# Loading one of twelve streamed weight blocks over eight DMA engines instead of sixteen

## The chip, the cores and the metric

The kernel runs on one core of a Trainium2 chip. The metric is the device time of one execution in microseconds; the time of a kernel is the median of its runs. The core has a matrix engine (PE), a vector engine (DVE), a scalar engine (ACT), a general engine (POOL), an engine that mainly issues transfers (SP), and sixteen DMA engines that move data between memory and the on-chip buffers for all of them.

## The reference, cut to what matters

Two independent parts are computed, and their outputs stand side by side in one output of 2048 rows and 2048 columns. Part A is an attention layer that runs over 64 segments one after the other, because each hands eight memory rows to the next. Part B is a long convolution by a state space model; the change doesn't touch it.

```python
for s in range(n_seg):                       # 64 segments of 32 rows
    xs = x[:, s * seg_len:(s + 1) * seg_len, :]
    h = concatenate([mem, xs], axis=1)       # 8 memory rows, 32 rows; 1024 wide
    q, k, v = (einsum('btd,dhe->bhte', h, W) for W in (Wq, Wk, Wv))   # 32 heads of 128
    p = softmax(where(mask, einsum('bhqe,bhke->bhqk', q, k) * scale, -1e9))
    o = einsum('bhte,hed->btd', einsum('bhqk,bhke->bhqe', p, v), Wo)
    mem = o[:, :8, :]
    outs.append(o[:, 8:, :])
```

The four weights Wq, Wk, Wv and Wo have 1024 x 4096 values each, 8 MB in bf16, and every segment needs all of them.

## The kernel before, in words

Part B runs first, to about 590 us. Beside it the kernel projects those rows of part A that no segment hands on, copies some weights, and loads others for good. Then part A's loop (`part_a`, `for s in range(NS)`) runs over the 64 segments.

The weights are cut into 64 blocks of 128 x 2048 values (512 KB). A key names a block: `("k", 0, 2)` is the third block of rows of the first half of Wk's columns, and `("o", 13)` holds rows 26 x 128 to 28 x 128 of Wo, that is two heads. Most blocks stay in on-chip memory for the whole loop (`W_res`), a few are kept in a bank for matmul results (`KEPT`), and twelve are read from memory again in every segment (`STREAM` and `STREAM_O`): three of k, two of q, four of v, and the output blocks 4, 8 and 13. In order of use a segment streams k(0,2), q(0,2), k(1,1), k(1,5), q(1,4), v(0,2), v(0,7), v(1,4), v(1,7), o4, o8, o13.

Streamed blocks are read from a copy in memory (`WD`), which `streamed_copies` makes once, during part B, as a contiguous 128 x 2048 array. `part_a.stage` (line 337) takes one of four buffers (`wst`, `SLOTS = 4`) in turn and issues the load on SP (line 340). The schedule is the program's order, written out by hand. SP goes ahead of the other engines in that order, so a load is issued as soon as SP has issued the one before it and PE has finished with the block that had the same buffer, four blocks earlier.

`unit(key)` (line 300) returns a block to whoever multiplies by it. `quads` (line 414) does the projections: four matmuls of 512 columns a block, on four groups of 32 columns of PE. `oproj` (line 527) does the output projection: eight matmuls of 256 columns a block. Block o13 is the last but one in the order of the final call, `oproj(pp[:, 1, :], (8, 10, 12, 14, 9, 11, 13, 15), o1)`, and the next streamed block after it is k(0,2), the second block of the next segment's k projection.

ACT issues the small transfers of a segment: `load_pk` (line 376) and `load_vx` (line 382), and in `stores` a 64 KB part to `OLd` (line 392) and the segment's 64 KB of output rows (line 396). The latter store writes through a view of four column groups (`"r (q d) -> q r d"`), so that its outermost size is 4.

After the loop, line 647 loads the output blocks that aren't resident once more, for the matmuls of line 664.

Of the kernel before, what the change touches and what calls it, by code (L numbers as in the profile page):

```python
# [10 lines left out]
BF16 = mybir.dt.bfloat16  # L11
# [13 lines left out]

STREAM = {("k", 0): (2,), ("q", 0): (2,), ("k", 1): (1, 5), ("q", 1): (4,), ("v", 0): (2, 7), ("v", 1): (4, 7)}
STREAM_O = (4, 8, 13)

BANK = {("k", 0): "b0", ("q", 0): "b1", ("k", 1): "b2", ("q", 1): "b0", ("v", 0): "b3", ("v", 1): "b2"}
KEPT = {("k", 0, 7): (("K7a", 0, 512), ("K7b", 512, 512), ("K7c", 1024, 512), ("K7d", 1536, 384), (None, 1920, 128)),  # L30
# [28 lines left out]
def streamed_keys():  # L59
    return [key for key in [(m, t, kc) for (m, t), kcs in STREAM.items() for kc in kcs] + [("o", u) for u in STREAM_O]]  # L60


def streamed_copies(ctx, tc, src):
    nc = tc.nc
    dram = ctx.enter_context(tc.tile_pool(name="a_wd", bufs=1, space=bass.MemoryType.DRAM))
    out, copies = {}, []
    for key in streamed_keys():
        t_ = dram.tile([128, 2048], BF16, name="WD_%s" % "_".join(str(i) for i in key))
        copies.append(lambda t_=t_, key=key: nc.sync.dma_start(
            out=t_[:].rearrange("e (h d) -> e h d", h=2) if key[0] == "o" else t_[:], in_=src(key)))  # L70
        out[key] = t_
    return out, copies


class Ahead:
# [3 lines left out]
    def __init__(self, ctx, tc, x, src, seg_len):  # L79
        self.nc, self.tc, self.x, self.src = tc.nc, tc, x, src  # L80
        self.S, self.Dm = x.shape
        self.SL, self.XM = seg_len, 24
        self.XL, self.KC, self.NS = seg_len - 24, self.Dm // 128, self.S // seg_len
        dram = ctx.enter_context(tc.tile_pool(name="a_dram", bufs=1, space=bass.MemoryType.DRAM))
        self.VXd = dram.tile([self.NS + 1, 128, 256 + self.KC * self.XM], BF16, name="VXd")
        self.PKd = dram.tile([self.NS, 128, 512], BF16, name="PKd")
        self.PVd = [dram.tile([self.NS * self.XL, 2048], BF16, name="PVd%d" % t) for t in range(2)]
        self.OLd = dram.tile([self.NS // 8, 128, 8 * 256], BF16, name="OLd")
# [183 lines left out]
def part_a(ctx, tc, x, src, WD, HE, seg_len, out_a, ahead, W_res, rest, places, first):  # L272
    nc = tc.nc
# [26 lines left out]
    def unit(key):  # L300
        if key in rest:

            rest.remove(key)
            load_resident(tc, wres, src, key, W_res, None, places.pop(0)() if places else None)
        if key in W_res:
            return W_res[key]
        if key in KEPT:
            return ahead_of.pop(key) + halves.get(key, [])
        between.pop(key, lambda: None)()
        if key in first:  # L310
            return first.pop(key)
        if key[0] == "v":
            for k_ in rest[0:3 if key[1] == 0 else 1]:
                rest.remove(k_)
                load_resident(tc, wres, src, k_, W_res)
        return stage(key, WD[key][:])

    ctx_l = ctx_w.enter_context(ExitStack())
    pers = ctx_l.enter_context(tc.tile_pool(name="a_pers", bufs=1))
# [14 lines left out]
    def words(out, in_):  # L334
        nc.vector.tensor_scalar(out=out.bitcast(I32), in0=in_.bitcast(I32), scalar1=0, scalar2=None, op0=ALU.bitwise_or)  # L335

    def stage(key, in_):
        t_ = wst.tile([128, 2048], BF16, name="wst", tag="w%d" % (loads[0] % SLOTS))
        loads[0] += 1
        nc.sync.dma_start(out=t_[:].rearrange("e (h d) -> e h d", h=2) if len(in_.shape) == 3 else t_[:], in_=in_)  # L340
        return t_

    def load_kept(key):
# [62 lines left out]
    for s in range(NS):  # L406
# [123 lines left out]
        a = quads("k", 0, (0, 2, 4, 6, 1, 3, 5, 7))  # L530
        k0 = evac(a, "k0")
        a = quads("q", 0, range(0, 6))
# [4 lines left out]
        a = quads("k", 1, range(0, 3))  # L537
# [16 lines left out]
        a = quads("q", 1, range(KC))  # L554
# [3 lines left out]
        a = quads("v", 0, range(0, 3))  # L558
# [34 lines left out]
        a = quads("v", 1, range(0, 5))  # L593
# [46 lines left out]
    wo = {}  # L640
    for u in order:
        if ("o", u) in W_res:
            wo[u] = W_res["o", u]
        else:
            wo[u] = spare.pop(0)
            if ("o", u) in WD:
                nc.sync.dma_start(out=wo[u][:], in_=WD["o", u][:])
            else:
                nc.sync.dma_start(out=wo[u][:].rearrange("e (h d) -> e h d", h=2), in_=src(("o", u)))
    stores(NS - 1, ob)  # L650
# [6 lines left out]
    for b in range(4):  # L657
        pe = [ps_k.tile([128, 512], F32, name="pe", tag="keep%d" % (2 * (b % 2) + n)) for n in range(2)]
        for u in order:
            for hh in range(2):  # L660
                h = 2 * u + hh
                hi = 16 * (h // 16) + 4 * (h % 4) + (h % 16) // 4
# [983 lines left out]
@with_exitstack  # L1646
def kernel(
    ctx: ExitStack,
    tc: tile.TileContext,
    A_x: bass.AP,  # L1650
    A_mem0: bass.AP,
    A_Wq: bass.AP,
    A_Wk: bass.AP,
    A_Wv: bass.AP,
    A_Wo: bass.AP,
    A_seg_len: bass.AP,
    B_u: bass.AP,
    B_A_re: bass.AP,
    B_A_im: bass.AP,
    B_B_re: bass.AP,  # L1660
    B_B_im: bass.AP,
    B_C_re: bass.AP,
    B_C_im: bass.AP,
    B_log_dt: bass.AP,
    B_Dskip: bass.AP,
    out: bass.AP,
):
    seg_len = int(A_seg_len)
    Dm = A_x.shape[2]
    Db = B_u.shape[2]  # L1670
    out_a = out[0, :, 0:Dm]
    out_b = out[0, :, Dm:Dm + Db]
    src = weight_blocks(A_Wq.rearrange("d h e -> d (h e)"), A_Wk.rearrange("d h e -> d (h e)"),
                        A_Wv.rearrange("d h e -> d (h e)"), A_Wo.rearrange("h e d -> (h e) d"))
    WD, copies = streamed_copies(ctx, tc, src)
    ahead = Ahead(ctx, tc, A_x[0], src, seg_len)
    ctx_w = ctx.enter_context(ExitStack())
    W_res, places, first = {}, [], {}
    rest = Keys(RESIDENT)
    rest.ctx = ahead.ctx = ctx_w  # L1680

    def residents(stay, early, uqs, last):
        def put(t_):
            load_resident(tc, None, src, rest.pop(0), W_res, None, t_)
        for _ in range(EARLY[0]):
            load_resident(tc, stay, src, rest.pop(0), W_res)
            yield
        def some(where, tag, n):
            t_ = where.tile([128, n, 2048], BF16, name="W%d" % n, tag=tag)
            return [t_[:, i, :] for i in range(n)]  # L1690
        for t_ in some(stay, "KT1", 2):
            put(t_)
            yield
        for t_ in early:
            put(t_)
            yield
        put(last[0])
        yield
        for t_ in uqs:
            put(t_)  # L1700
            yield
        ahead.wst = ctx_w.enter_context(tc.tile_pool(name="a_wst", bufs=1, side="right"))
        pool = ctx_w.enter_context(tc.tile_pool(name="a_wre0", bufs=1, side="right"))
        for _ in range(EARLY[1]):
            load_resident(tc, pool, src, rest.pop(0), W_res)
            yield
        for i, key in enumerate([("k", 0, 7)] + streamed_keys()[0:SLOTS - 1]):
            first[key] = t_ = ahead.wst.tile([128, 2048], BF16, name="wst", tag="w%d" % i)
            tc.nc.sync.dma_start(out=t_[:], in_=WD[key][:] if key in WD else src(key))
            yield  # L1710
        for i in [c // 2 for c in PAIRS]:
            places.append(lambda i=i: stay.tile([128, 2048], BF16, name="W1", tag="MI%d" % i))
        for i in range(LATE):
            put(places.pop(0)())
            yield
        put(last[1])
        yield

    low = low_blocks(ctx, tc)
    ahead.low = low.pop()  # L1720
    copies += [lambda t_=t_: load_resident(tc, None, src, rest.pop(0), W_res, None, t_) for t_ in low]

    def first_state(m0, xt):
        nc = tc.nc
        consts = constants(tc, ahead)
        hT = next(consts)
        nc.sync.dma_start(out=xt[:].rearrange("p k r -> p (k r)"), in_=ahead.VXd[0, :, 256:])
        nc.sync.dma_start(out=m0, in_=A_mem0[0])
        pm = yield
        for kc in range(8):  # L1730
            nc.tensor.transpose(out=pm[:, kc, :], in_=m0[:, kc * 128:(kc + 1) * 128], identity=ahead.consts[0][0:8, 0:8])
        nc.vector.tensor_copy(out=hT[:, :, ahead.XM:], in_=pm)
        nc.gpsimd.tensor_copy(out=hT[:, :, 0:ahead.XM], in_=xt[:])
        yield
        next(consts)
        yield

    with ExitStack() as ctx_b:
        part_b(ctx_b, tc, B_u[0], B_A_re, B_A_im, B_B_re, B_B_im, B_C_re, B_C_im, B_log_dt, B_Dskip, out_b, ahead, copies, residents, first_state)
    with ExitStack() as ctx_a:  # L1740
        part_a(ctx_a, tc, A_x[0], src, WD, A_Wo.shape[0] * A_Wo.shape[1], seg_len, out_a, ahead, W_res, rest, places, first)
# [35 lines left out]
```

## Time and profile before

| what | value |
|---|---|
| median of 3 runs | 1962.2 us (1956.45, 1962.97, 1962.2) |
| span of the profiled execution, first to last instruction | 1954.2 us |
| the profiled execution's own time | not given apart from its span |
| PE busy | 1810.2 us, 93% |
| DVE, ACT, POOL busy | 71%, 48%, 23% |
| moved by DMA | 591.08 MB, mean 302 GB/s |
| mean granted clock of PE | 0.974 |

Instructions, their engines and their tiles are shown under the line of the kernel that issued them ("L340"). A tile name stands for all buffers of that name: `wst` for the four buffers of streamed blocks, `WD_o` for the copies of the three output blocks, `acc` and `pp` for results of the projections. "SPq" is SP's queue of transfers, q1 holds the transfers that SP issues, q10 those of ACT, q0 those of POOL, and q8 fetches instructions. A line of the page that shows 40 digits cuts the span into 40 slices of 48.9 us, and a digit is the busy share of a slice in tenths.

### The profile page before, as it was taken

How to read it: one execution, taken by the hardware profiler on the slowest of the kernel's cores; microseconds unless marked ns; L12 is line 12 of the kernel's file. 1: busy time of each engine (PE TensorE's matmuls, PEld its weight loads, DVE VectorE, ACT ScalarE, POOL GpSimd, SP SyncE). 2: the span in 40 equal slices, each digit the busy share in tenths (PEclk: the TensorE clock that was granted, in tenths of full speed). 3: DMA queues.
4: the chain of work that ended last, by engine and by line, in shares of the span. 5: the costliest groups of instructions: out<-in, count | busy, mean ns of one | idle time of the engine just before them, and what ended most of it. 6: DMA issues, size and time to landing. Idle time of an engine off the chain costs nothing.

```text
span 1954.2 us, 74192 instructions
## 1 busy us (share of the span) xinstructions
PE 1810.2 (93%) x31750; PEld 1106.9 (57%) x31788; DVE 1379.4 (71%) x3431; ACT 934.7 (48%) x1670; POOL 443.1 (23%) x855
## 2 busy tenths in 40 slices
PE   8999999887997899999999999999999999998998
PEld 3666666556775555555555555555555555555554
DVE  8599989889994566666676766676766676666650
ACT  8799989851122334344434443444444444444320
POOL 2364545223222111111111111111111111111120
PEclk8999999878998999999999999999999999999999
DMA  7889898867589999999999999999999999999991
GB/s 222 243 232 283 237 287 243 221 188 253 169 272 334 347 340 340 340 339 336 355 339 346 345 335 336 339 341 350 344 350 334 347 341 347 339 350 324 338 343 30
DMA packets 337342, 591.08 MB, mean 302 GB/s; under 512 B 94848, under 2 KB 211048, under 8 KB 334964
## 3 DMA queue, kind: packets, MB, share of 16 engines
q1 hardware_dynamic: 284824, 531.85, 79.9%
q10 hardware_dynamic: 45532, 29.57, 4.9%
q0 software_dynamic: 6656, 24.92, 3.5%
q8 instruction: 249, 4.08, 0.8%
q14 instruction: 81, 0.66, 0.1%
HBM read 528.78 MB, written 68.47 MB: 306 GB/s over the span
## 4 chain that ended last, share of the span: by engine, by line
PE 37%; DMA 27%; DVE 4%; issue 1%; ACT 1%; POOL 0%; SPq 0%; ACTq 0%; DVEq 0%; POOLq 0%
PE acc L414 20%; DMA wst<-WD_v 8%; PE pp L527 8%; DMA wst<-WD_o 7%; DMA wst<-WD_k 3%; DMA arena<-PKd 3%; DMA wst<-WD_q 3%; PE pe L664 3%; PE tr L425 2%; DMA out_dram<-arena 1%; DMA out_dram<-uu 1%; PE pv L495 1%; PE pv L499 1%; DVE arena L621 1%; PE sc L439 1%
## 5 line engine op out<-in xcount | busy, mean ns | idle before, releaser
L414 PEld LDWEIGHTS <-a_hT 128*32 128x32 bf16 x12352 | 328.4, 96 | 324.0 <-issue 64.0
L420 ACT CAST arena<-acc 128x512 bf16<-128x512 f32 x384 | 224.8, 585 | 404.3 <-PE acc L414 324.5
L414 PE MATMUL acc<-wst,a_hT 128*32 128x512 bf16 x2304 | 229.5, 382 | 34.2 <-DMA wst<-WD_v 22.9
L527 PEld LDWEIGHTS <-arena 128*32 128x32 bf16 x8256 | 216.1, 96 | 73.2 <-issue 49.3
L335 DVE TENSOR_SCALAR arena<-keep 128x256 int32<-128x256 int32 (+1 forms) x512 | 175.6, 395 | 28.1 <-PE acc L414 28.0
L428 POOL COPY arena<-arena 128x128 bf16<-128x128 bf16 x128 | 37.3, 292 | 683.0 <-DMA arena<-PKd 314.4
L414 PE MATMUL acc<-XM,a_hT 128*32 128x512 bf16 x2560 | 172.7, 380 | 0.0
L458 ACT ACTIVATE sc<-sc 128x160 f32<-128x160 f32 (+1 forms) x192 | 63.9, 333 | 127.6 <-DVE sc L455 127.6
L454 DVE TENSOR_REDUCE a_mx<-sc 128x4 f32<-128x160 f32 (+1 forms) x192 | 71.7, 374 | 74.7 <-PE sc L442 73.3
L197 PE MATMUL pro<-XM,wsl 128*128 128x512 bf16 x480 | 117.7, 383 | 5.3 <-DVE kst L206 2.2
L527 PE MATMUL pp<-W_o,arena 128*32 128x256 bf16 x3584 | 120.6, 273 | 0.1
L414 PE MATMUL acc<-W,a_hT 128*32 128x512 bf16 x1536 | 120.0, 384 | 0.0
L542 DVE COPY arena<-tr 128x512 bf16<-128x512 bf16 x64 | 27.2, 425 | 128.8 <-PE tr L425 128.8
L462 DVE TENSOR_REDUCE a_mx<-sc 128x4 f32<-128x160 f32 (+1 forms) x192 | 72.9, 379 | 55.3 <-ACT sc L458 54.9
L489 POOL TENSOR_TENSOR arena<-arena,a_BD 128x128 bf16<-128x128 bf16 x128 | 51.1, 399 | 231.1 <-DVE arena L472 229.7
L1266 DVE TENSOR_SCALAR nr<-ptt 128x456 f32<-128x456 int16 x128 | 80.4, 628 | 31.8 <-PE ptt L1244 29.0
L1258 ACT ACTIVATE E<-pa 128x648 bf16<-128x648 f32 x128 | 87.7, 712 | 18.1 <-PE pa L1250 16.0
L414 PE MATMUL acc<-wq,a_hT 128*32 128x512 bf16 x1024 | 92.2, 381 | 0.0
L414 PE MATMUL acc<-g,a_hT 128*32 128x512 bf16 x1024 | 90.4, 379 | 0.0
L1459 POOL TENSOR_TENSOR Bt<-ev 128x512 bf16<-128x512 f32 x32 | 55.7, 1760 | 150.2 <-DVE ev L1456 150.2
L621 ACT CAST arena<-pp 128x128 bf16<-128x128 f32 x64 | 17.0, 265 | 149.8 <-DVE arena L621 149.8
L425 PEld LDWEIGHTS <-arena 128*128 128x128 bf16 x1024 | 57.8, 98 | 54.4 <-issue 45.1
(339 smaller groups left out, 4071.3 us busy)
## 6 DMA issues: line engine op xcount, KB each, us to landing
wst<-WD_v SPq DMA_DIRECT2D x256, 512.0 KB
wst<-WD_k SPq DMA_DIRECT2D x192, 512.0 KB
wst<-WD_o SPq DMA_DIRECT2D x192, 512.0 KB
wst<-WD_q SPq DMA_DIRECT2D x128, 512.0 KB
Ud<-ux POOLq DMA_DIRECT2D x16, 1024.0 KB, 8.2
wq<-Ud SPq DMA_DIRECT2D x32, 512.0 KB
wsl<-in_A_Wk_dram SPq DMA_DIRECT2D x16, 512.0 KB
wsl<-in_A_Wv_dram SPq DMA_DIRECT2D x16, 512.0 KB
```

Source lines behind the costliest of these rows:

```text
L197: nc.tensor.matmul(a[:], lhsT=w[:, kc, 128 * j:128 * j + 128], rhs=xTl[:, kc, :, :].rearrange("p s k -> p (s k)"), start=(kc == 0), stop=( ...
L335: nc.vector.tensor_scalar(out=out.bitcast(I32), in0=in_.bitcast(I32), scalar1=0, scalar2=None, op0=ALU.bitwise_or)
L414: nc.tensor.matmul(a[32 * g:32 * g + 32, o_:o_ + rhs.shape[1]], lhsT=hT[:, kc, :], rhs=rhs, start=(kc == 0), stop=(kc == KC - 1), tile_pos ...
L420: nc.scalar.copy(out=q, in_=a[:])
L425: nc.tensor.transpose(out=p[:, hl, :, :].rearrange("p a b -> p (a b)"), in_=q[:, 128 * hl:128 * hl + 128], identity=ident[:])
L454: nc.vector.tensor_reduce(out=m_, in_=x, axis=AX.X, op=ALU.max)
L458: nc.scalar.activation(out=flat(sc, i), in_=flat(sc, i), func=ACT.Exp, scale=scale)
L462: nc.vector.tensor_reduce(out=m_, in_=x, axis=AX.X, op=ALU.add)
L527: nc.tensor.matmul(po[32 * qt:32 * qt + 32, o_:o_ + rhs.shape[1]], lhsT=oT[:, h % 4, (h % 16) // 4, :], rhs=rhs, start=False, stop=(h == 3 ...
L664: nc.tensor.matmul(pe[n][:], lhsT=left[2 * b + hi // 16][:, 128 * (hi % 16):128 * (hi % 16) + 128], rhs=wo[u][:, 1024 * hh + 512 * n:1024 ...
L1258: sc.activation(out=T["E", r, e // 4][:, lo:lo + 8 * NE].rearrange("p (i c) -> p i c", i=2), in_=T.pop(("p", r, e))[:, :, 0:4 * NE], func= ...
L1266: v.tensor_scalar(out=T["n", r, e // 4][:, lo:lo + 8 * NT], in0=T.pop(("t", r, e))[:, 0:8 * NT].bitcast(I16)[:, 0:16 * NT:2], scalar1=floa ...
```

## The change

A class `Streamed` takes the place of the plain copy of a streamed block. For eleven of the twelve blocks it makes the same 128 x 2048 array, the same copy and the same load. For `("o", 13)` a table gives `(128, 8)`: 128 rows over 8 engines. The copy is then an array of eight portions; each holds 16 rows of 2048 values, and 2048 values (4096 B) are left unused behind each. The copy and both loads (in the loop and after it) read or write it through a view of 8 x 16 x 2048, so that the outermost size of that side is 8. The other side of the load is the buffer's 128 rows, as before.

```diff
+PORTIONS = {("o", 13): ((128, 8),)}
...
+PITCH = 2048
+
+class Streamed:
+    def __init__(self, dram, nc, src, key):
+        self.nc, self.src, self.key, self.pieces = nc, src, key, []
+        lo = 0
+        for i, (rows, engines) in enumerate(PORTIONS.get(key, ((128, 16),))):
+            name = "WD_%s_%d" % ("_".join(str(j) for j in key), i)
+            each = rows // engines
+            if key in PORTIONS:
+                t_ = dram.tile([engines, each * 2048 + PITCH], BF16, name=name)
+                ap = t_[:, 0:each * 2048].rearrange("a (b f) -> a b f", f=2048)
+            else:
+                ap = dram.tile([128, 2048], BF16, name=name)[:]
+            self.pieces.append((lo, lo + rows, ap))
+            lo += rows
...
+    def copy(self):
+        for lo, hi, ap in self.pieces:
+            flat = ap if len(ap.shape) == 2 else None
+            w = self.src(self.key)[lo:hi]
+            if self.key[0] == "o":
+                w = w.rearrange("(a b) h d -> a b h d", a=ap.shape[0]) if flat is None else w
+                out = ap.rearrange("a b (h d) -> a b h d", h=2) if flat is None else ap.rearrange("e (h d) -> e h d", h=2)
...
+            self.nc.sync.dma_start(out=out, in_=w)
+
+    def load(self, t_):
+        for lo, hi, ap in self.pieces:
+            self.nc.sync.dma_start(out=t_[lo:hi, :], in_=ap)
...
-    def stage(key, in_):
+    def stage(key):
         t_ = wst.tile([128, 2048], BF16, name="wst", tag="w%d" % (loads[0] % SLOTS))
         loads[0] += 1
-        nc.sync.dma_start(out=t_[:].rearrange("e (h d) -> e h d", h=2) if len(in_.shape) == 3 else t_[:], in_=in_)
+        WD[key].load(t_)
         return t_
...
             if ("o", u) in WD:
-                nc.sync.dma_start(out=wo[u][:], in_=WD["o", u][:])
+                WD["o", u].load(wo[u])
```

In the built programs the order of instructions is the same on every engine. In the load of block 13 the source goes from 128 x 2048 to 8 x 16 x 2048.

More of the change, by code (lines that the diff above doesn't have):

```diff
@@ L60, in streamed_keys @@
     return [key for key in [(m, t, kc) for (m, t), kcs in STREAM.items() for kc in kcs] + [("o", u) for u in STREAM_O]]
+PITCH = 2048
[13 more added lines that the diff above has]
+            lo += rows
+        assert lo == 128
+    def copy(self):
[5 more added lines that the diff above has]
+                out = ap.rearrange("a b (h d) -> a b h d", h=2) if flat is None else ap.rearrange("e (h d) -> e h d", h=2)
+            else:
+                w = w.rearrange("(a b) f -> a b f", a=ap.shape[0]) if flat is None else w
+                out = ap
+            self.nc.sync.dma_start(out=out, in_=w)
+    def load(self, t_):
+        for lo, hi, ap in self.pieces:
+            self.nc.sync.dma_start(out=t_[lo:hi, :], in_=ap)
 def streamed_copies(ctx, tc, src):
-    nc = tc.nc
     dram = ctx.enter_context(tc.tile_pool(name="a_wd", bufs=1, space=bass.MemoryType.DRAM))
[L66 to L72, printed above, removed]
+    out = {key: Streamed(dram, tc.nc, src, key) for key in streamed_keys()}
+    return out, [w.copy for w in out.values()]
 class Ahead:
@@ L315, in unit @@
                 load_resident(tc, wres, src, k_, W_res)
-        return stage(key, WD[key][:])
+        return stage(key)
     ctx_l = ctx_w.enter_context(ExitStack())
@@ L1708, in residents @@
             first[key] = t_ = ahead.wst.tile([128, 2048], BF16, name="wst", tag="w%d" % i)
-            tc.nc.sync.dma_start(out=t_[:], in_=WD[key][:] if key in WD else src(key))
+            if key in WD:
+                WD[key].load(t_)
+            else:
+                tc.nc.sync.dma_start(out=t_[:], in_=src(key))
             yield
```

## The prediction

> **What bounds the kernel now.** I read the page first (busy slices, then the chain of waits), then the windows of the steady loop, its DMA queues, the waits of PE and of SP's queue, and a piece of the chain in order of time.
>
> ```profile
> PE   8999999887997899999999999999999999998998
> DMA  7889898867589999999999999999999999999991
> GB/s 222 243 232 283 237 287 243 221 188 253 169 272 334 347 340 340 340 339 336 355 339 346 345 335 336 339 341 350 344 350 334 347 341 347 339 350 324 338 343 30
> ...
> PE 37%; DMA 27%; DVE 4%; issue 1%; ACT 1%; POOL 0%; SPq 0%; ACTq 0%; DVEq 0%; POOLq 0%
> ```
>
> From slice 13 on (about 636 us, part A's loop) PE and the DMA engines are both at nine tenths or more; the chain is shared by these two.
>
> ```profile
> core 0: us, PE busy (x) PEld busy (x) DVE busy (x) ACT busy (x) POOL busy (x), PEclk, DMA share, GB/s
> 900.00:1100.00 200.00, 192.16 (x4158) 113.62 (x4158) 135.94 (x426) 83.75 (x184) 31.88 (x82) 1.00 0.97 344
> 1500.00:1700.00 200.00, 190.55 (x4090) 110.92 (x4086) 132.64 (x413) 84.11 (x184) 31.67 (x81) 1.00 0.95 343
> ```
>
> The clock is 1.00 here, so no throttling enters. One segment is one lap. The 192 loads of output blocks run from 636.1 to 1886.8 us, 64 laps of three, so a lap takes about (1886.8 - 636.1) / 63.7 = 19.6 us. PE is busy 852 of the 900 us from 900 to 1800, 18.6 us of a lap; 1.0 us is idle.
>
> ```profile
> q1 hardware_dynamic: 79201, 288.40, 88.6%
> q10 hardware_dynamic: 25929, 17.33, 6.1%
> q8 instruction: 144, 2.36, 1.0%
> ...
> wst<-WD_o SPq DMA_DIRECT2D x137, 512.0 KB
> ```
>
> This is the DMA view of 900 to 1800 us. SP's queue moves 288.40 MB, 70,400 packets of 4096 B (the other records are 4 B completions), in 88.6% of 16 x 900 us: 181 ns a packet. In the packet records an undisturbed one lasts 159 ns and the next on its engine starts 155 ns after it; about 4% last over 300 ns, up to 2.1 us, and make up the difference. All queues together fill 95.8%; without the 4 ns that neighbours overlap (2.5%) it is about 93.4%. An engine is idle 6.6%, 1.3 us of a lap.
>
> ```profile
> SPq L340 <- PE acc L414: 340.5, 376, 3.1
> SPq L340 <- DMA wst<-WD_v: 116.7, 188, 3.6
> ```
>
> SP's queue spends its time waiting for PE to release one of four buffers. In the waits of the engines (us in total, times, longest), PE in turn waits for blocks:
>
> ```profile
> PE acc L414 <- DMA wst<-WD_v: 22.9, 25, 5.4
> ```
>
> ```profile
> 1002.87 6.89 DMA wst<-WD_k
> 1009.76 0.04 issue
> 1009.80 0.42 PE acc L414 x4
> 1010.24 6.49 DMA wst<-WD_v
> ```
>
> A closed loop: a block takes 6 to 7 us from issue to its last completion because about four are queued, PE uses it in 0.4 us, and that frees the next issue. A block is complete when its slowest engine is, so the pace is that of the most loaded engines, with PE only 1.0 us a lap behind.
>
> **The change, part by part.** PE, ACT, DVE and POOL keep their instructions and order; on SP the order is unchanged too. What changes is the shape of 64 loop loads, of one copy and of one load at the end.
>
> *The loop load of block 13.* Its source is now eight portions of 16 rows, its destination 128 rows; it is confined to eight engines. Each of engines 0 to 7 gets 16 packets where it had 8, engines 8 to 15 none. Bytes, packet size and count stay the same. The nearest row is the store of segment rows, whose outermost size is 4: the trace records about four data completions for each, against 16 for a streamed block. [...]
>
> Per lap, engines 0 to 7 carry 8 x (181 - 4) = 1.42 us more and engines 8 to 15 1.42 us less. A lap of a lower engine has 12 x 8 = 96 block packets now and 104 then; an upper engine 88. Bounds for the lap: if the idle 1.3 us is fully usable, it lengthens by 1.42 - 1.30 = 0.12 us; if none is, by 1.42 us. Over 64 laps that is 8 to 91 us. I take 1.2 us, near the upper end: the idle arises because an engine that is ahead waits for an issue that waits for PE, which waits for the slowest engine. That wait doesn't go away when the load rises; only the scatter among eight engines instead of sixteen helps a little. 64 x 1.2 = 77 us. What is late next: k(0,2) and q(0,2) of the next segment, queued on engines 0 to 7 behind block 13, then PE's matmuls on them, then SP's wait for their buffers. The upper eight get ahead and idle.
>
> *Issue on SP.*
>
> ```profile
> L340 SPq DMA_DIRECT2D wst<-WD_o x192: 319/320/1162, 636.1 to 1886.8; - x192
> L396 ACTq DMA_DIRECT2D out_dram<-arena x63: 547/556/1144, 651.0 to 1873.1; - x63
> ```
>
> Flat loads take SP 320 ns; the store, with a three-step side like the new load, takes ACT 556 ns. So +0.24 us an issue, 15 us over 64 if all of it showed. Queued behind it on SP is only the next load, which waits for PE's release anyway, and the engines still have earlier blocks queued when block 13 is issued. I take 0, and 15 us as the price if the engines have run dry.
>
> *The copy and the last load.* Each once: 16 more packets of 2 KB an engine (84 ns undisturbed in the records), 1.3 us, beside part B's work at 317 us; and 8 more of 4 KB, 1.4 us, at 1889 us under the last segment's output. 0, at most 2.7 us.
>
> *The 4096 B between portions* changes only where eight streams read. The long packets cost (181 - 159) x 128 = 2.8 us of engine time a block, 0.35 us on each of eight engines. No row shows one layout against another: from -0.35 us a lap (22 us, all long packets of this block gone) to +0.35 us. I take 0.
>
> Sum: 77 us. The profiled execution's span is 1954.2 us, 8.0 us (0.4%) under the median 1962.2 us; 2031 us in its terms, about 2039 us for the median.
>
> **Rivals.** *The upper eight set the pace now (faster).* If the 6.6% idle all lies on engines 0 to 7, they have 2.6 us free a lap and the upper ones nothing; moving 1.42 us then relieves the binding engines. The gain is held by what is left below, 2.6 - 1.42 = 1.2 us, and by PE's 1.0 us: up to 64 us, half of it 32 us, giving 1930 us. It decides once the upper engines carry over 1.42 us a lap more than the lower. Against it: the 16 completions of a streamed block spread evenly (medians after the first: eighth 0.73, ninth 0.82, fifteenth 1.53, last 1.99 us), with no step between two groups of eight, and the store already adds 32 packets of 512 B, 0.74 us a lap, to its four engines. For it: no view names engines, and 2.36 MB of instruction fetches (144 packets of about 1 us) may sit on upper ones.
>
> *The idle absorbs it (no change).* 1.30 free against 1.42 added leaves 8 us at 0.12 us a lap, and 2 us is gone in the scatter: 1962 to 1970 us. Against it: DMA waits already reach PE (22.9 us for WD_v alone).
>
> *Writes collide (slower still).* With 16 neighbouring rows an engine, engines may write where others write, while the upper ones go on with the next block. The price is up to twice 159 ns a packet: 16 x 159 = 2.5 us a lap, 163 us on top; with half of it, 80 us, 2120 us. [...] No row here shows that collision.
>
> *The change doesn't do what it says:* if the load still ran on 16 engines, only the issue's 0 to 15 us would remain. The store's four completions speak against that; it goes with "no change".
>
> **How the numbers follow.** A measurement of this kernel can tell about 0.3% (6 us) from no change. Forecast (1970 to 2055 us) 0.55, collisions 0.17, upper eight 0.22, absorbed or not done 0.06. The forecast is 2039 us. Faster 0.22, same 0.06, slower 0.72. Leaving out the better half of the "upper eight" case and the worse half of the collisions, the range is 1930 to 2110 us.
>
> **What would show it.** Right: laps of 20.5 to 21.2 us in the loop, PE's share down to about 0.89, DMA share down to about 0.90, more PE wait on WD_k, WD_q and WD_o, block 13's issue near 0.56 us, and 8 completions for it. Collisions: packets near 318 ns around block 13 and laps over 21.5 us. Wrong: laps under 19.6 us with a higher DMA share and shorter waits of SP on wst; that would say that engines 8 to 15 were the late ones. Laps unchanged would say that the idle could be used after all.

## The result, and the profile after

The changed kernel takes 2234.4 us (median; 2226.7 to 2248.4) against 1961.1 us for the kernel before on the same chip: 1.1411 times as long, 95% interval 1.1367 to 1.1455, or 273 us more. The forecast was 2039 us, its range ended at 2110 us. The direction was right; 77 us were forecast where 273 came. The profiled execution spans 2225.0 us, 270.8 us more than before.

The page after: the slices and the chain of waits.

```profile
PE   8999998789868888888888888888888788788879
PEclk9999998789989889989999999999999999989999
DMA  7889988675898888888888888889888888888892
GB/s 222 249 242 275 255 252 232 193 250 172 288 337 275 274 273 286 283 283 290 288 281 276 288 281 278 283 278 286 287 274 273 279 289 284 276 261 273 285 300 72
...
PE 38%; DMA 34%; DVE 1%; issue 1%; ACT 0%; SPq 0%; DVEq 0%; ACTq 0%
PE acc L446 28%; DMA wst<-WD_o 26%; DMA wst<-WD_v 7%; PE pe L696 2%; PE tr L457 2%; PE pp L559 2%; PE tro L659 1%; DVE arena L653 1%; PE sc L471 1%; DMA out_dram<-uu 0%; PE yp L1543 0%; ACT arena L653 0%; PE sc L474 0%; DMA uu<-in_B_u_dram 0%; DMA arena<-VXd 0%
```

The loop moves about 280 GB/s where it moved about 343, and both PE and the DMA engines fell from nine tenths to eight. The second line of the chain names the place: the output blocks (`WD_o`) now hold 26% of the span, PE's projections (L446) 28%. In the kernel before that line had 7% for `WD_o` and 20% for the projections (there L414):

```profile
PE acc L414 20%; DMA wst<-WD_v 8%; PE pp L527 8%; DMA wst<-WD_o 7%; DMA wst<-WD_k 3%; DMA arena<-PKd 3%; DMA wst<-WD_q 3%; PE pe L664 3%; PE tr L425 2%; DMA out_dram<-arena 1%; DMA out_dram<-uu 1%; PE pv L495 1%; PE pv L499 1%; DVE arena L621 1%; PE sc L439 1%
```

Both grew, the DMA engines by about 229 us of chain (34% of 2225.0 against 27% of 1954.2) and PE by about 122 us, a first sign that there are two causes.

The same windows as before:

```profile
core 0: us, PE busy (x) PEld busy (x) DVE busy (x) ACT busy (x) POOL busy (x), PEclk, DMA share, GB/s
900.00:1100.00 200.00, 171.32 (x3439) 95.27 (x3435) 112.88 (x350) 71.91 (x156) 27.30 (x69) 0.93 0.89 287
1500.00:1700.00 200.00, 171.39 (x3380) 94.34 (x3369) 112.38 (x351) 69.85 (x153) 27.89 (x69) 0.92 0.89 283
```

PE does 17% fewer instructions in a window but is busy only 10 to 11% less: the granted clock is 0.92 to 0.93 where it was 1.00. The issues of output blocks run from 638.0 to 2154.1 us, so a lap takes 23.8 us by the prediction's division, 4.2 us more than before. From one issue of block 13 to the next it is 24.0 us, against 19.75 us.

The DMA view of 900 to 1800 us:

```profile
q1 hardware_dynamic: 65016, 237.87, 82.9%
q10 hardware_dynamic: 21107, 14.11, 5.0%
```

SP's queue moves 18% fewer bytes (288.40 MB before) but keeps the sixteen engines busy only 6% less (88.6% before): the mean packet of 4096 B rose from 181 to about 206 ns (0.829 x 16 x 900 us over 58,074 packets). Engines are idle more than before, and what they do takes longer.

The waits, of SP's queue and then of the engines:

```profile
SPq L98 <- PE acc L446: 515.5, 380, 3.4
SPq L98 <- DMA wst<-WD_o: 327.6, 178, 5.2
```

```profile
PE pp L559 <- DMA wst<-WD_o: 200.1, 97, 4.5
PE acc L446 <- DMA wst<-WD_v: 22.9, 24, 5.1
```

and the first of them in the kernel before:

```profile
PE pp L527 <- DMA wst<-WD_o: 8.8, 18, 1.3
```

PE's wait for `WD_v` is what it was. The wait for an output block was 8.8 us in the kernel before and is 200.1 us now, 3.1 us a lap. SP's issue of block 13 takes 599 ns (320 before). Of its completions one comes 1.0 us after the issue and eight follow from the engines, the last at 8.9 us (median); before, sixteen came between 3.4 and 5.3 us.

The packet records show what happens meanwhile. Between 5 and 6.5 us after the issue of block 13, nine tenths of all packets of 4096 B, those of the other blocks included, last over 250 ns; their median is 318 ns, and half of them lie between 288 and 366 ns. Before, most took 159 ns there. Over the loop 26% of the packets of 4096 B take over 170 ns (7% before).

A piece of the chain in order of time (start, us, what):

```profile
1098.66 7.54 DMA wst<-WD_o
1106.20 0.04 issue
1106.24 0.68 PE pp L559 x14
...
1107.88 5.77 PE acc L446 x74
...
1121.16 9.87 DMA wst<-WD_o
```

A lap of the chain now has one long transfer, of an output block, and then a long run of PE's work, where the piece before that the prediction shows is a string of transfers of 6 to 7 us with 0.4 us of PE between them.

PE's timeline around the end of a lap, in the kernel after (start, us, instruction, and in brackets the idle time before it):

```profile
1106.24 0.40 PE L559 MATMUL pp<-wst,arena 128*32 128x256 bf16 x8 [2.44 <-DMA wst<-WD_o]
...
1108.63 1.07 PE L446 MATMUL acc<-W_k,a_hT 128*32 128x512 bf16 x8
1109.49 1.07 PE L446 MATMUL acc<-Wlow,a_hT 128*32 128x512 bf16 x8
...
1111.11 0.60 PE L446 MATMUL acc<-W_q,a_hT 128*32 128x512 bf16 x8
```

and the same matmuls in the kernel before:

```profile
1102.13 0.60 PE L414 MATMUL acc<-W_k,a_hT 128*32 128x512 bf16 x8
1102.56 0.61 PE L414 MATMUL acc<-Wlow,a_hT 128*32 128x512 bf16 x8
```

PE waits 2.44 us for block 13, and from 1.4 us after the end of that wait its matmuls run at half speed for some 3 us: eight of them take 1.07 us instead of 0.60. The window of these matmuls has a granted clock of 0.50 (the value ahead of the DMA share):

```profile
1107.60:1111.00 3.40, 3.40 (x33) 1.33 (x37) 1.70 (x7) 0.36 (x2) 0.00 (x0) 0.50 0.91 308
```

The clock records of the traces have 59 stretches at half clock in the changed loop, 49 of them 3.41 us long, 235 us together; in the kernel before there are 2 after 630 us, 12 us together. In the groups by line, the mean matmul on `W_k` rose from 379 to 565 ns, on `Wlow` from 383 to 561 ns (first the kernel before, then after):

```profile
L414 PE MATMUL acc<-W_k,a_hT 128*32 128x512 bf16 x768 | 63.9, 379 | 0.0
L446 PE MATMUL acc<-W_k,a_hT 128*32 128x512 bf16 x768 | 97.0, 565 | 0.0
```

The 270.8 us of the span are 90.6 us more PE busy time (1900.8 against 1810.2 us) and 180.2 us more PE idle time.

### The profile page after: what moved, and what is told of

Same layout as the page of the kernel before. It is cut to its first block, busy times and chain, and to the rows that moved or that the text cites. A ratio compares the mean times of both kernels' runs of the same rounds, so it can differ in the third digit from the quotient of the medians.

```text
span 2225.0 us, 74192 instructions
## 1 busy us (share of the span) xinstructions
PE 1900.8 (85%) x31750; PEld 1122.2 (50%) x31788; DVE 1382.2 (62%) x3431; ACT 935.7 (42%) x1670; POOL 447.8 (20%) x855
## 4 chain that ended last, share of the span: by engine, by line
PE 38%; DMA 34%; DVE 1%; issue 1%; ACT 0%; SPq 0%; DVEq 0%; ACTq 0%
PE acc L446 28%; DMA wst<-WD_o 26%; DMA wst<-WD_v 7%; PE pe L696 2%; PE tr L457 2%; PE pp L559 2%; PE tro L659 1%; DVE arena L653 1%; PE sc L471 1%; DMA out_dram<-uu 0%; PE yp L1543 0%; ACT arena L653 0%; PE sc L474 0%; DMA uu<-in_B_u_dram 0%; DMA arena<-VXd 0%
## 5 line engine op out<-in xcount | busy, mean ns | idle before, releaser
L446 PEld LDWEIGHTS <-a_hT 128*32 128x32 bf16 x12352 | 335.6, 103 | 386.0 <-issue 130.4
L559 PEld LDWEIGHTS <-arena 128*32 128x32 bf16 x8256 | 221.9, 98 | 282.7 <-issue 257.9
L446 PE MATMUL acc<-wst,a_hT 128*32 128x512 bf16 x2304 | 240.7, 406 | 23.8 <-DMA wst<-WD_v 22.9
L559 PE MATMUL pp<-wst,arena 128*32 128x256 bf16 x1536 | 79.0, 282 | 210.7 <-DMA wst<-WD_o 200.1
L446 PE MATMUL acc<-XM,a_hT 128*32 128x512 bf16 x2560 | 172.2, 380 | 0.0
L653 DVE CAST arena<-pp 128x128 bf16<-128x128 f32 x64 | 18.7, 292 | 243.3 <-PE pp L559 243.3
L559 PE MATMUL pp<-W_o,arena 128*32 128x256 bf16 x3584 | 125.3, 279 | 0.2 <-issue 0.2
L446 PE MATMUL acc<-W,a_hT 128*32 128x512 bf16 x1536 | 118.8, 385 | 0.0
L446 PE MATMUL acc<-W_k,a_hT 128*32 128x512 bf16 x768 | 97.0, 565 | 0.0
L446 PE MATMUL acc<-Wlow,a_hT 128*32 128x512 bf16 x768 | 96.6, 561 | 0.0
```

Of the source, the lines that this page charges most:

```text
L446: nc.tensor.matmul(a[32 * g:32 * g + 32, o_:o_ + rhs.shape[1]], lhsT=hT[:, kc, :], rhs=rhs, start=(kc == 0), stop=(kc == KC - 1), tile_pos ...
L559: nc.tensor.matmul(po[32 * qt:32 * qt + 32, o_:o_ + rhs.shape[1]], lhsT=oT[:, h % 4, (h % 16) // 4, :], rhs=rhs, start=False, stop=(h == 3 ...
L653: (nc.scalar.copy if j else nc.vector.tensor_copy)(out=osb[:, 128 * j:128 * j + 128], in_=pp[:, 1, 128 * j:128 * j + 128])
```

## The experiments

Four theories were set against each other. W: engines that write certain rows at the same moment share a way into the on-chip memory, and their packets take longer. S: reading from a source in portions is slow. I: a load with a three-step side is slow to issue or to describe. L: the uneven number of packets on the engines is all there is. The lower engines are, in what follows, the eight that a load of eight portions uses, the upper ones the other eight: the trace shows eight completions for block 13 (sixteen before), but no view names an engine or the rows that it writes. That they are the same eight each time, and which rows an engine writes in a load without portions, is the author's assumption. Each edit is against the changed kernel unless it says otherwise. The kernel before was measured again beside each group (1957.0 to 1962.8 us); ratios are to it.

**The gap.** The distance between portions goes from 4096 to 256 B.

```diff
-PITCH = 2048
+PITCH = 128
```

> As after the change, with 256 B between the portions and not 4096 B. W, L and I: 2234 us within 15 us, the same packets. S: another time, by 50 us or more in either direction.

Measured 2230.6 us, ratio 1.138 (1.124 to 1.152). The same as the changed kernel: where the eight streams read plays no part.

**Rows apart in the source.** Block 13 is loaded without portions over sixteen engines, but each row of its copy is followed by 4096 B that are not used.

```diff
-PORTIONS = {("o", 13): ((128, 8),)}
+PORTIONS = {}
...
-                ap = dram.tile([128, 2048], BF16, name=name)[:]
+                ap = dram.tile([128, 4096 if key == ("o", 13) else 2048], BF16, name=name)[:, 0:2048]
```

> Block 13 over sixteen engines by a flat load as before, from a copy with 4096 B behind each row of 4096 B. W, L and I: 1962 us within 6 us. S, if any gap in the source costs: over 1980 us, long packets around block 13.

Measured 1973.3 us, ratio 1.0062 (1.0039 to 1.0086): 11 us, a little over the 6 us that were allowed, and far from the 273 us. So gaps in the source are not the cause. That portions as such are slow to read is excluded by the quarters in the streams below; with them S falls.

**Sixteen portions.** Sixteen runs of eight rows, still 4096 B apart, so all sixteen engines have 8 packets.

```diff
-PORTIONS = {("o", 13): ((128, 8),)}
+PORTIONS = {("o", 13): ((128, 16),)}
```

> Block 13 from a copy in sixteen portions of 8 rows with 4096 B between them, over sixteen engines: the portions, the gap and the three-step side stay, the uneven load goes. W: if the rows go to the engines in runs of 8 neighbours, pairs of engines still meet, packets near 318 ns around block 13 and 2000 to 2100 us; if they are spread as in a flat load, 1962 us. S: still slow, about 2234 - 77 = 2157 us. I: 1962 to 1977 us. Theory L (the uneven load alone): 1962 us, normal packets.

Measured 2047.0 us, ratio 1.0442 (1.0343 to 1.0542), 85 us. No engine has more packets than before, so L alone cannot be the whole; between 3 and 5 us after the issue 60 to 66% of the packets last over 250 ns. The issue takes 520 ns. PE's clock hardly enters here: the mean matmul on `W_k` takes 390 ns.

**Four quarters.** Four loads of 32 rows, each in eight portions of four rows.

```diff
-PORTIONS = {("o", 13): ((128, 8),)}
+PORTIONS = {("o", 13): ((32, 8),) * 4}
```

> Block 13 in four loads of 32 rows, each over eight engines, so an engine writes 4 neighbouring rows a load and not 16; engines 0 to 7 carry the same 16 packets as after the change. Theory W (writes collide: engines that write neighbouring rows at the same time share a way into the on-chip memory): the eight loads of one piece no longer meet each other, only the upper engines' next block, so the lap falls from 24.0 to 21 to 22.5 us, 2040 to 2140 us, and packets over 250 ns around block 13 fall from 0.9 to under 0.5. Theory S (the source in eight portions is slow to read): the portions are smaller but of the same kind, 2200 to 2260 us. Theory I (a load with a three-step side is slow to issue or to describe): four such loads instead of one, 2234 us or more.

Measured 2136.5 us, ratio 1.0899 (1.0780 to 1.1018). The lower engines have the same 16 packets of block 13 as in the changed kernel, there are four times as many three-step issues, and it is 98 us faster. What differs is which rows are written at one time, and with the wait the clock: the mean matmul on `W_k` takes 512 ns, not 565. The long packets fell less than W had it: at most 77% of them last over 250 ns in any half microsecond, against 93%, not under half.

**Loads one at a time.** A kernel that computes nothing of the reference and loads blocks singly, each after the one before has landed.

> Nothing of the reference is computed: the kernel only loads blocks of 4096 B rows, each load waiting for the one before, and copies one block to the output; its whole time says nothing. What is read is the time of a packet by kind of load. Theory W (engines that write certain pairs of rows at the same moment share a way into the on-chip memory): 128 rows without gaps over sixteen engines about 159 ns a packet, as in the kernel before; 128 rows as sixteen runs of eight rows, or as eight runs of sixteen, about 300 ns (two engines to a way) although nothing else is under way; 32 rows as eight runs of four about 159 ns; two engines alone, engine 0 on rows 0 to n-1 and engine 1 on rows n to 2n-1: about 159 ns at some of the distances n = 2, 4, 8, 16, 32, 64, and about 300 ns at others, so that a map of the ways comes out of it. Rival L (only the number of packets of an engine counts): 159 ns in all of them, and the load over eight engines takes 16 x 159 = 2.5 us from its first packet to its last. Rival S (reading from a source in portions is slow): every load from portions is slow, the 32 rows in eight portions too, whatever the distance of the rows. In groups of three loads back to back, W: the two flat blocks around an eight-engine load have packets near 300 ns as well; L: 159 ns.

Mean packet (median of five loads) 183 ns without portions, 232 in sixteen runs, 234 in eight runs, 213 in a quarter over eight engines. Two engines alone: 169 ns a packet with their rows 64 apart, 201 ns with rows 32 apart, 203 to 244 ns at smaller distances, where the loads are short and their start weighs most. Without the first microsecond of each load it is 161 to 167 ns for 64 rows, 178 to 198 for 32 and 163 to 198 for 16, so these pairs give no map. There was no doubling. A single load doesn't keep its engines writing all at once: a plain one takes 1.8 to 1.9 us from its first packet to its end, where eight packets of 159 ns would take 1.3 us. That sixteen runs take 232 ns and plain loads 183, with 8 packets on each engine in both, speaks against L, but W isn't settled by it.

**Streams of loads.** The same with sixteen loads back to back (nothing of the reference is computed). "low" writes rows 0 to 63 in two quarters over the eight lower engines and rows 64 to 127 in one load over sixteen; "high" exchanges the two halves.

> Nothing of the reference is computed: streams of 16 loads of 128 rows of 4096 B, issued back to back into 16 tiles, three times for each kind; each stream waits until the one before has landed. Read are the time from a stream's first packet to its last and the mean time of a packet. Theory W (engines that write certain rows at the same moment share a way): flat loads over sixteen engines 16 x 8 x 159 ns = 20 us and up to 24 us with their start; sixteen runs of eight rows, same engines and packets, 35 to 42 us with packets near 300 ns; eight runs of sixteen rows 40 us if only the number of packets counted, and at least 60 us with shared ways; quarters of 32 rows over eight engines faster than eight runs of sixteen rows. Where every fourth load is one over eight engines, the flat loads beside it have long packets too. Low (rows 0 to 63 over the eight lower engines, rows 64 to 127 over sixteen) is faster than high (rows 64 to 127 over the eight lower engines) when mixed with flat loads, since the two differ in nothing but the rows that the eight engines write. Rival L (only packets an engine counts): runs of eight rows as flat, 20 to 24 us; half, quarters 40 us each; low and high equal, 30 us. Rival I (loads in three steps are slow to describe to the engines): runs, half, quarters all take long by the same factor, packets stay near 159 ns with idle time between them, low and high equal.

The windows of single streams, all of the same 8.4 MB: without portions, sixteen runs, quarters, then every fourth load low, every fourth high.

```profile
core 0: us, DVE busy (x) POOL busy (x), PEclk, DMA share, GB/s
76.50:99.50 23.00, 2.20 (x14) 0.00 (x0) 1.00 0.94 365
160.80:195.20 34.40, 2.32 (x14) 0.00 (x0) 1.00 0.99 244
404.50:451.50 47.00, 2.24 (x14) 0.00 (x0) 1.00 0.48 178
1137.50:1169.30 31.80, 2.37 (x15) 0.00 (x0) 1.00 0.88 263
1243.00:1279.00 36.00, 2.39 (x15) 0.00 (x0) 1.00 0.89 233
```

Sixteen runs keep the same sixteen engines 99% busy and move a third less: 0.99 x 16 x 34.4 us / 2048 = 266 ns a packet, against 0.94 x 16 x 23 / 2048 = 169 ns. Quarters are three-step loads too and their packets take 0.48 x 16 x 47 / 2048 = 176 ns, so neither the form of the load nor its source in portions is it; I falls. Mixed with plain loads, low took 28.7 to 32.7 us over its three streams and high 35.6 and 36.0 in the two that nothing else ran beside. In these streams low and high issue their three loads in the same order. Low and high alone took the same (38 to 41 us). W's 60 us for eight runs came in one stream of three: they took 65, 54 and 43 us, the last with a median packet of 159 ns. The same load can be slow or nearly undisturbed, as W would have it if the engines get out of step; no run here forced that.

**Low rows against high rows in the loop.** Block 13 in three loads, 12 packets on each lower engine and 4 on each upper one in both kernels.

```diff
-PORTIONS = {("o", 13): ((128, 8),)}
+PORTIONS = {("o", 13): ((32, 8), (32, 8), (64, 0))}    # low
+PORTIONS = {("o", 13): ((64, 0), (32, 8), (32, 8))}    # high
```

(0 stands for a load without portions.)

> Block 13 in three loads: rows 0 to 31 and 32 to 63 each in eight portions of four rows over the eight lowest-numbered engines, rows 64 to 127 in one load without portions over sixteen. The lower engines carry 12 packets of block 13, the upper 4. Theory W: half the unevenness (25 to 50 us) and few collisions, if the rows that the lower engines write here are those that they write in a flat load as well: 1985 to 2030 us. Rivals without rows (unevenness and the form of the load alone): the same time as the load with high and low rows exchanged, within 15 us.

> The same with the rows exchanged: rows 64 to 95 and 96 to 127 in portions over the eight lowest-numbered engines, rows 0 to 63 in one load over sixteen. Theory W: the lower engines now write rows that the upper engines write in the flat loads around it, so at least 30 us over the load with low rows: 2030 to 2090 us. Rivals without rows: the same as with low rows, within 15 us.

Low 2076.5 us, ratio 1.0607 (1.0536 to 1.0678); high 2119.9 us, 1.0811 (1.0748 to 1.0874). Packets on each engine, sizes, number of issues and forms are the same, and the intervals don't meet: 43 us come with the exchange of the rows. In the loop the exchange also turns the order round (low issues the 64 rows without portions last, high first); no run separates the two here, but in the streams, where the order is the same, high is slower too. Part of the 43 us goes through PE's clock: the mean matmul on `W_k` takes 439 ns with low and 470 with high. Both came out above what W expected (2030 and 2090 us at most); both still have two more issues and an uneven load.

**Unevenness alone.** Block 13 is loaded as before the change; beside it 64 rows are copied from device memory to device memory, over eight engines or over sixteen.

```diff
-PORTIONS = {("o", 13): ((128, 8),)}
+PORTIONS = {}
...
+            self.nc.sync.dma_start(out=self.extra[1], in_=self.extra[0])   # [8, 8, 2048] or [16, 4, 2048]
```

> Block 13 is loaded as in the kernel before, over sixteen engines; beside it, once a lap, 64 rows of 4096 B are copied from device memory to device memory over the eight lowest-numbered engines, 8 packets on each. The lower engines so carry the same 8 packets more a lap as in the changed kernel, but write no more into the on-chip memory. Theory W: the unevenness has its own price, that of the prediction's sum, 8 x 181 ns or 1.4 us a lap less what the engine's idle time covers: 1990 to 2060 us, and the packets of the streamed blocks stay near 180 ns. Rival L (the unevenness alone makes the 273 us): 2200 to 2250 us.

> The same copy of 64 rows over sixteen engines, 4 packets on each: the control of the copy over eight. If an engine's number of packets sets the lap, 4 x 181 ns or 0.7 us a lap less idle time: 1965 to 2010 us, about half of what the copy over eight adds. If the copy costs by its bytes in device memory rather than by engine, the same as the copy over eight.

Eight engines: 2061.2 us, ratio 1.0502 (1.0452 to 1.0552), 101 us. Sixteen: 2006.2 us, ratio 1.0237 (1.0206 to 1.0268), 46 us. The same bytes cost 55 us more on half the engines, and the packets of the streamed blocks keep their mean (179 ns). So 8 more packets on the lower engines cost 101 us, with the copy's own issue and traffic in it. The 55 us are for moving four packets from the upper engines to the lower; the change moves eight, 110 us if it is twice as much (an estimate). The slow clock hardly enters: the mean matmul on `W_k` takes 389 ns with the copy over eight.

**The store spread out** (against the kernel before): the 32 small packets a lap on each of four engines (the prediction's four completions) are meant to go to all sixteen.

```diff
-            nc.scalar.dma_start(out=rows, in_=ob[:, 0, :])
+            for q in range(4):
+                nc.scalar.dma_start(out=rows[q], in_=ob[32 * q:32 * q + 32, 0, :])
```

> The kernel before, with the store of a segment's 32 output rows issued as four transfers of 32 rows each, so that its 128 packets of 512 B lie on sixteen engines, 8 on each, in place of 32 on each of the four lowest-numbered. If unevenness of the engines costs as the prediction's sum has it, the four engines lose up to 0.5 us of packets a lap: 1925 to 1960 us. If the lower four do not set the lap, 1955 to 1965 us; three more issues on ScalarE a lap could cost up to 3 x 0.3 us a lap if they were on the path: up to 2020 us.

Measured 2017.7 us, ratio 1.0281 (1.0237 to 1.0325): slower. ACT issues four stores a lap where it issued one, and 87.1 us of its waits are now on its own `OLd` stores; which part of the 57 us is that, and which the changed DMA traffic, stays open.

**PE's clock.** Idle matmuls, 24 or 40 a lap, ahead of those that wait for block 13; their result is read by nobody.

```diff
                 w = unit(("o", u))
+                if u == 13:
+                    for _ in range(24):
+                        nc.tensor.matmul(pp[:, 0, 128:256], lhsT=ident[:], rhs=ident[:], start=False, stop=False, skip_group_check=True)
```

> The changed kernel with 24 idle matmuls (128 x 128 by 128 x 128, into part of an accumulator that nobody reads) a lap on PE, just ahead of the matmuls that wait for block 13; they take about 24 x 70 ns = 1.7 us of the 2 to 3 us for which PE waits there, so that they delay nothing as long as the wait is longer. Theory K (a part of the loss is the clock that is granted after that wait: the next lap's first matmuls took 561 to 565 ns in place of 380 in the changed kernel, and PE's busy time rose by 91 us): with PE busy during the wait the clock stays up, the matmuls on W_k and Wlow fall to below 450 ns, and the time falls by 30 to 90 us: 2140 to 2205 us. Rival D (the lap is set by the DMA engines alone; slower matmuls only shorten the next wait): the matmuls get faster, the wait for block 13 longer, 2220 to 2250 us. If the clock does not follow PE's idling: 560 ns as before and 2230 us or more.

> The same with 40 idle matmuls, about 2.8 us, as long as the mean wait for block 13. Theory K: the clock is held up at least as well, but where the wait was shorter than 2.8 us the block's matmuls are delayed: 2140 to 2230 us, PE's wait for block 13 close to nothing. Rival D: 2220 to 2260 us.

24 matmuls: 2186.6 us, ratio 1.113 (1.108 to 1.118). 40 matmuls: 2165.3 us, 1.103 (1.098 to 1.109). Useless work made the changed kernel 48 and 69 us faster, as theory K had it. With 40, PE's wait for an output block and the first projections in the groups by line (busy, mean ns, idle time before):

```profile
L446 PE MATMUL acc<-W_k,a_hT 128*32 128x512 bf16 x768 | 70.2, 410 | 0.0
L446 PE MATMUL acc<-Wlow,a_hT 128*32 128x512 bf16 x768 | 70.1, 408 | 1.6 <-issue 1.4 <-DVE a_hT L664 0.2
L562 PE MATMUL pp<-wst,arena 128*32 128x256 bf16 x1536 | 76.9, 276 | 65.7 <-DMA wst<-WD_o 59.7 <-DVE arena L497 2.5 <-DVE arena L367 1.4
```

Matmuls of `W_k` over 500 ns are 72% in the changed kernel, 35% with 24 idle matmuls, 12.5% with 40 and none in the kernel before; the stretches at half clock fall from 59 to 34 and 12. Two details missed: with 24 the mean on `W_k` is 471 ns, not below 450, and with 40 PE still waits 59.7 us for output blocks, not close to nothing. So the slow clock is a cause of time, not only a companion of a lap that the DMA engines set: rival D falls.

## Why the prediction was right or wrong

*The bound and the place: right.* The loop was bound by the transfers with PE just behind, and what came late was block 13 and the blocks queued behind it. The direction, the 8 completions, the longer issue (forecast 0.56 us, measured 0.60 us; at most 18 us over the loop, and whether it is hidden was not measured by itself) and the DMA share (about 0.90 forecast, 0.89 measured) held. PE's share was to be 0.89 and is 0.86; the laps were to be 20.5 to 21.2 us and are 23.8 us. One reading was off: the 852 us of PE's busy time belong to 1000 to 1900 us; from 900 to 1800 us it is 858 us, so PE idled 0.9 us a lap. That changes nothing in the sum.

*The sum's one term, 77 us for the uneven load: near, a little small.* The copies put it at about 100 us (101 measured, 110 by doubling 55), or less if a part of that is the copy's own; the full 1.42 us a lap would be 91 us. What failed is that the sum ended there.

*"Writes collide": the failing step.* It was told as a rival with a chance of 0.17 and priced at half of its bound. The two signs that the prediction set for it both came: packets near 318 ns around block 13 (a median of 318 ns between 5 and 6.5 us after its issue) and laps over 21.5 us (23.8 us). It also touches more than the eight engines' own 16 packets: the nine tenths over 250 ns there include packets of the other blocks in flight. That the time hangs on the rows is shown: low rows cost 43 us less than high rows in the loop, and 28.7 to 32.7 us against 35.6 and 36.0 in the streams, where the order is the same; the two engines alone, 169 ns a packet 64 rows apart and 201 at 32, agree only weakly. By what the packets get long then is not shown, and the factor of two in the price was the author's estimate. Nothing in the trace before excluded the collisions, and half of their price, 80 us, was more than the whole sum of 77 us: they should have moved from a rival into the sum. With an even load and hardly any slow clock, rows in sixteen runs alone cost 85 us.

*"The clock is 1.00 here, so no throttling enters": the second failing step.* That was read from the kernel before, in which PE hardly waits. The change makes it wait 2 to 3 us at one place of each lap, and in most laps the clock is then halved for some 3 us at the start of the next, on the path (59 stretches at half clock in 64 laps). This is worth at least 69 us, the gain of the 40 idle matmuls, which leave 12 such stretches and a clock of 0.98 in windows of the loop where it was 0.92 to 0.93. In the timeline above, a wait of 2.44 us, with short stalls behind it, was enough: 1.07 us for eight matmuls against 0.60. How long a wait must be for that, no run shows.

*The parts together.* About 100 us are unevenness and at least 69 us the clock; 273 less these leaves about 100 us for the rows. That remainder was not measured by itself in the loop: the nearest are 85 us for a whole block in sixteen runs and 43 us for exchanging half a block. The parts also feed each other, since the clock falls because of the wait. The exact split stays open.

*Rivals.* "The upper eight set the pace" is wrong: the same copy on the lower eight alone costs 55 us more than on all. "The idle absorbs it" is wrong by the same run. "The change doesn't do what it says" is ruled out by the completions. The gap, taken as nothing within 22 us either way, was nothing: 2230.6 against 2234.4 us.

*The range* ended at 2110 us because it left out the worse half of the collisions (even their middle price, 2120 us, lay outside it) and had no term for the clock. The full collision price with the uneven load was 77 + 163 us, 2202 us; with the clock's 69 us it would have been 2271 us, a little above what was measured. That this comes so near is partly luck: the collision price counted only the eight engines' own packets.

## What to carry to other kernels

When a transfer is confined to fewer engines, count not only packets an engine but also which rows each engine writes at a time, and beside which other transfers: as far as the runs can split it, the rows cost about as much here as the uneven load. When a change makes PE wait at one place of a loop, look at the clock of the matmuls behind that place; here a clock of 1.00 in the profile before fell to 0.92 once PE had to wait. If a rival that speaks against a change has a price and nothing in the trace excludes it, as here with collisions priced at up to 163 us, the price belongs into the sum.

## What the runs showed of the hardware

- A load of 128 rows in sixteen runs of eight neighbouring rows took 266 ns a packet, and a plain load of the same block 169 ns, both with the sixteen engines 94 to 99% busy, in streams with nothing else under way.
- One load of 512 KB in eight runs of sixteen rows had slow packets of other blocks beside it: between 5 and 6.5 us after its issue nine in ten of all packets of 4096 B were over 250 ns, where most had taken 159 ns.
- With a wait of 3.1 us a lap for an output block, PE had half its clock in 59 stretches of the loop's 64 laps, 49 of them 3.41 us long. 40 matmuls whose result nobody reads, put into that wait, left 12 such stretches and took 69 us off a kernel of 2234 us.
- The distance between portions in device memory made no difference (2230.6 us with 256 B, 2234.4 us with 4096 B), and 4096 B behind each row cost 0.6% (1973.3 us).
